# Windowed attention: half-empty key blocks multiplied by the values as pairs of 128x64 array tiles

## The chip, the core and the metric

The kernel runs on one core of one Trainium2 chip. A core has five engines that run at the same time, each through its own list of instructions in order: TensorE (PE, the 128x128 matrix array; the loads of its stationary operand are shown as PEld), VectorE (DVE), ScalarE (ACT), GpSimd (POOL) and SyncE (SP, which here only starts transfers). They synchronise by semaphores. The metric is the device time of one execution in microseconds, taken as the median of several runs. Lower is better.

## What is computed

Four residual layers over x of 2048 tokens by 512 features, in the order A, B, A, B. Both kinds start with a layernorm, have 32 heads of 16 features, and end with a product with `wo` that is added to x. Layer A is linear attention (no mask, all tokens). Layer B is softmax attention in a window of 256 tokens:

```python
x = x + _A_ref(_layernorm(x, axis=-1), A_wqkv, A_wo)
x = x + _B_ref(_layernorm(x, axis=-1), B_wqkv, B_wo)
x = x + _A_ref(_layernorm(x, axis=-1), A_wqkv, A_wo)
x = x + _B_ref(_layernorm(x, axis=-1), B_wqkv, B_wo)
...
# in _B_ref
scores = jnp.einsum("bhqd,bhkd->bhqk", q, k) * (Dh ** -0.5)
mask = (idx[:, None] - idx[None, :] >= 0) & (idx[:, None] - idx[None, :] < W)
scores = jnp.where(mask[None, None], scores, -1e9)
p = _softmax(scores, axis=-1)
o = jnp.einsum("bhqk,bhkd->bhqd", p, v)
```

## The kernel before

The program is a list of operations (`Op`), each with an engine, an emitting function and the tiles it reads and writes. A compressed table in the source (`TABLE`, unpacked in `place`) gives the order of all 2541 operations, the engine of each one that could go to several, and the PSUM bank of each PSUM tile (8 banks of 128 partitions by 512 f32). `synchronise` then derives every semaphore wait from that order. So each engine, and SP's queue of transfers, has a fixed order written out in the table, and nothing is decided at run time.

Tokens are cut into 16 tiles of 128. Layer 1 (A) is built by `layer_a_keys`; layers 2 and 4 (B) by `middle`, in which work of the neighbouring A layers is spread: the output of the A layer before (`a_out`, L406), layernorms (DVE and POOL, then a transposing transfer on SP's queue), and, in layer 2, keys, values and queries of layer 3. `barrier` holds the sums over all tokens that stand between.

In a B layer, for every tile j of 128 tokens:

- `b_qkv` (products L420) makes queries and keys, `b_v` (L406) the values. The keys and values are kept as blocks of 64 keys, and a 128-row operand holds a block for two heads, whose rows alternate. There are therefore 16 head pairs, numbered by f (0 to 3) and gq (0 to 3), and two key blocks, 2j and 2j+1, in each tile.
- `b_scores` (L638, row tiles of 32x128 of the array, four at once) multiplies the key block with up to 256 query columns, and `b_far` (L712 in layer 2, L715 in layer 4, the latter as 32x64 tiles, eight at once) with the last 64 columns of the window. ACT takes the exponential into the buffer P of probabilities (`pb`, `vp`; L648 and L725). The mask is a product or a select on DVE or POOL (L657, L658, L735, L743, L744).
- `b_values` (L764) multiplies probabilities by values. Its stationary operand is a 128x128 piece of P (two heads by 64 keys in the rows, 128 queries in the columns), the moving one 34 columns: 16 value features and a column of ones for each of the two heads. For the 128 queries of tile j, six key blocks matter: 2j-4 to 2j+1. Of the first, only the first 64 queries can see anything, and of the last only the last 64; P holds 64 columns of zeros beside both, so that all six are multiplied as full 128x128 operands. One tile takes 6 x 16 = 96 matmuls, in four operations called `pv` (one for each f, of 24), two of them into one bank.
- DVE divides by the sums (`rcp` L775, `div` L776), the result is transposed (L377 on SP's queue), multiplied by `wo` (L406) and added to x (L574).

The tiles j = 0 and 1 have fewer blocks, and the last tile of layer 4 has its own `b_values_end`. Line numbers are those of the kernel before; in the changed kernel lines from L749 on are moved down.

## Time and profile before

| | |
|---|---|
| median of 3 runs | 408.16 us (406.51 to 409.1) |
| profiled execution, first to last instruction | 405.4 us |
| instructions | 18074 |
| matmuls on PE, busy | 7930, 386.1 us (95%) |
| ACT busy | 341.5 us (84%) |
| DVE busy | 333.6 us (82%) |
| POOL busy | 149.2 us (37%) |

The page gives the span of the profiled execution, and no device time of its own for it; the median of the timed runs is 2.8 us above the span. Busy time is the union of what an engine executes; the matmuls overlap one another, so what one costs is read from start to start, not from its duration. A row of the timeline gives the start, the length from the first start to the last end, and the number of instructions in it. In the rows `128*128`, `32*128` or `32*64` are the rows and columns of the array tile that an instruction uses.

### The profile page before, as it was taken

The numbers are of one execution on the slowest core, as the hardware profiler recorded it, in microseconds if no ns is written. First come the engines' busy times: TensorE is split into PE (matmuls) and PEld (weight loads), VectorE is DVE, ScalarE is ACT, GpSimd is POOL, SyncE is SP. The second block draws the span as 40 slices with busy tenths as digits, with TensorE's granted clock in tenths as the row PEclk, the third lists the DMA queues.
The fourth block names the chain that finished last, engine by engine and source line by source line (L and its number), as shares of the span: only waits on it lengthen the run. The fifth ranks groups of instructions, "written<-read, shape, count | busy, mean of one in ns | idle before, by whom it ended". The sixth has DMA issues, their size and how long they took to land.

```text
span 405.4 us, 18074 instructions
## 1 busy us (share of the span) xinstructions
PE 386.1 (95%) x7930; PEld 263.9 (65%) x8004; DVE 333.6 (82%) x759; ACT 341.5 (84%) x439; POOL 149.2 (37%) x243
## 2 busy tenths in 40 slices
PE   8999999998999999999999999999999999999896
PEld 3644776766576566666666777677767775566665
DVE  6998898979998798887858789997898759776775
ACT  2655568998999999999998445999999999999994
POOL 3555624534363545541752213141132221232212
PEclk9999999999999999999999999999999999999999
DMA  8734216333253545353232000335224433344443
GB/s 250 243 66 128 82 41 127 106 80 92 71 94 69 122 97 101 63 129 81 62 79 56 20 2 12 96 83 135 69 57 108 110 76 75 82 118 94 115 124 107
DMA packets 67062, 37.75 MB, mean 93 GB/s; under 512 B 47688, under 2 KB 62152, under 8 KB 66984
## 3 DMA queue, kind: packets, MB, share of 16 engines
q1 hardware_dynamic: 66640, 35.67, 36.3%
q8 instruction: 63, 1.03, 1.2%
q0 software_dynamic: 336, 0.92, 0.7%
q14 instruction: 15, 0.12, 0.1%
q10 hardware_dynamic: 8, 0.00, 0.0%
HBM read 6.29 MB, written 2.10 MB: 21 GB/s over the span
## 4 chain that ended last, share of the span: by engine, by line
PE 76%; ACT 16%; DVE 5%; issue 2%; DMA 1%; ACTq 0%
PE ps L406 25%; PE ps L420 19%; PE ps L764 13%; ACT pb L648 10%; PE ps L638 6%; PE ps L481 3%; PE ps L715 2%; ACT pb L725 2%; ACT vp L648 2%; PE ps L712 1%; DMA xT<-xn 1%; PE ps L1067 1%; ACT vp L725 1%; PE ps L457 1%; DVE XQ L563 1%
## 5 line engine op out<-in xcount | busy, mean ns | idle before, releaser
L648 ACT ACTIVATE pb<-ps 128x1024 bf16<-128x1024 f32 (+3 forms) x224 | 198.4, 974 | 7.1 <-PE ps L638 5.5
L764 PEld LDWEIGHTS ps<-vB,pb 128*128 128x128 bf16 x2496 | 75.2, 96 | 10.4 <-issue 3.9
L764 PE MATMUL ps<-vB,pb 128*128 128x34 bf16 x2496 | 80.2, 177 | 0.3 <-DVE pb L744 0.2
L420 PE MATMUL ps<-xT,wBp 128*128 128x128 bf16 x1024 | 68.5, 219 | 0.9 <-DMA xT<-xn 0.6
L420 PEld LDWEIGHTS ps<-xT,wBp 128*128 128x128 bf16 x1024 | 58.8, 98 | 10.9 <-issue 4.5
L429 ACT ACTIVATE tE<-ps 128x512 bf16<-128x512 f32 x64 | 37.6, 605 | 26.3 <-PE ps L406 16.5
L743 POOL TENSOR_SCALAR_AFFINE_SELECT pb<-pb 128x1024 bf16<-128x1024 bf16 x32 | 36.9, 1152 | 53.8 <-DVE pb L735 37.6
L657 POOL TENSOR_SCALAR_AFFINE_SELECT pb<-pb 128x512 bf16<-128x512 bf16 x51 | 34.3, 673 | 48.4 <-ACT pb L648 20.6
L725 ACT ACTIVATE pb<-ps 128x1024 bf16<-128x1024 f32 x50 | 49.3, 1052 | 2.0 <-PE ps L715 1.0
L574 DVE TENSOR_TENSOR xres<-ps,xres 128x512 bf16<-128x512 f32 x63 | 42.9, 682 | 9.4 <-PE ps L406 9.1
L370 POOL TENSOR_TENSOR rs<-ve,negh 128x1 f32<-128x1 f32 x64 | 37.2, 581 | 32.1 <-DVE ve L369 27.5
L638 PE MATMUL ps<-XQ,kB 32*128 32x256 bf16 (+3 forms) x992 | 47.0, 264 | 1.7 <-ACT pb L648 0.5
L406 PE MATMUL ps<-wA,XQ 128*128 128x512 bf16 x179 | 45.7, 379 | 1.8 <-issue 0.8
L367 DVE BATCH_NORM_STATS2 stats<-xres 128x6 f32<-128x512 bf16 x64 | 43.8, 686 | 2.7 <-DMA xres<-in_A_x_dram 1.8
L420 PE MATMUL ps<-XQ,wA 128*128 128x128 bf16 x512 | 35.4, 219 | 0.1
L369 POOL TENSOR_SCALAR ve<-mv 128x1 f32<-128x1 f32 x45 | 11.5, 255 | 64.4 <-DVE mv L368 62.4
L420 PEld LDWEIGHTS ps<-XQ,wA 128*128 128x128 bf16 x512 | 30.6, 98 | 5.5 <-issue 0.7
L406 PE MATMUL ps<-wBv,xT 128*128 128x512 bf16 x108 | 30.1, 380 | 2.9 <-issue 1.4
L638 PEld LDWEIGHTS ps<-XQ,kB 32*128 32x128 bf16 x992 | 14.9, 92 | 26.4 <-ACT pb L648 8.4
L406 PE MATMUL ps<-wBo,oT 128*128 128x512 bf16 x103 | 28.6, 380 | 3.1 <-issue 1.9
L406 PE MATMUL ps<-M,XQ 128*128 128x512 bf16 x114 | 29.7, 380 | 1.3 <-issue 0.6
L406 PEld LDWEIGHTS ps<-wA,XQ 128*128 128x128 bf16 x192 | 17.0, 97 | 19.6 <-issue 2.1
(128 smaller groups left out, 569.1 us busy)
## 6 DMA issues: line engine op xcount, KB each, us to landing
vB<-vS SPq DMA_DIRECT2D x64, 136.0 KB, 2.6
kB<-vp SPq DMA_DIRECT2D x64, 128.0 KB, 2.2
wA<-in_A_wqkv_dram SPq DMA_DIRECT2D x3, 512.0 KB, 5.0
out_dram<-xres SPq DMA_DIRECT2D x9, 128.0 KB, 2.8
xres<-in_A_x_dram SPq DMA_DIRECT2D x2, 512.0 KB, 4.9
pb<-in_B_wqkv_dram SPq DMA_DIRECT2D x1, 1024.0 KB, 5.6
out_dram<-xres POOLq DMA_DIRECT2D x7, 128.0 KB, 2.2
xres<-in_A_x_dram SPq DMA_DIRECT2D x3, 256.0 KB, 4.7
```

The source lines that it names most:

```text
L367: self.on("DVE", "stats", lambda e: e.bn_stats(K.stats[:, t, :], K.xres[:, t, :]), key, dve(512), rd=[("xres", t)], wr=[("stats", t)])
L370: self.pow = self.on("POOL", "pow", lambda e: e.tensor_tensor(K.rs[:, t, :], K.ve[:, t, :], K.negh[:], ALU.pow), key + 0.03, (640, 690), r ...
L406: m = e.matmul(K.ps(ps), lhs(c), rhs(c), start=c == 0, stop=c == 3)
L420: m = e.matmul(K.ps(ps)[:, f * P:(f + 1) * P], w(c, f), xT(c), start=c == 0, stop=c == 3)
L429: self.on("ACT", "E", lambda e: e.activation(K.tE[:, s, :], K.ps(ps), ACT.Exp, bias=0.0), key, act(512), wr=[("tE", s)], ps=[ps])
L574: self.on("DVE", "res", lambda e: e.tensor_tensor(K.xres[:, t, :], K.ps(po), K.xres[:, t, :], ALU.add), key, dve(512), rd=[("xres", t)], w ...
L638: m = e.matmul(K.ps(ps[gq])[:, ns * i:ns * i + ns], K.kB[rows, j % 4, 2 * f + b, :, :], K.XQ[rows, f, q:q + ns], start=True, stop=True, ti ...
L648: return e.activation(out(h, ns).rearrange("p (f g) c -> p f g c", f=n), i, ACT.Exp, bias=0.0, scale=0.25)
L657: return e.affine_select(out=x, in_=x, compare_op=ALU.is_ge, fill=0.0, base=1, pattern=[[0, 4 * n], [2, 64]], channel_multiplier=-1)
L725: return e.activation(o.rearrange("p (f g) b c -> p f g b c", g=2), i, ACT.Exp, bias=0.0, scale=0.25)
L743: return e.affine_select(out=x, in_=x, compare_op=ALU.is_ge, fill=0.0, base=-2, pattern=[[0, 16], [-2, 64]], channel_multiplier=1)
L764: m = e.matmul(K.ps(ps)[:, 34 * u:34 * u + 34], K.P((b // 2) % rp)[:, f, gq % 2 * 2 + gq // 2, o:o + P], K.vB[:, (b // 2) % 4, b % 2, r, : ...
```

## The change

For every tile j from 2 on (but for the last of layer 4), `b_pairs` takes the place of `b_values`. The four key blocks that all 128 queries may see, 2j-3 to 2j, are multiplied as before, as full 128x128 operands: four operations of 16 matmuls. The two half-empty blocks are multiplied as pairs: the first 64 queries with block 2j-4 on the array's columns 0 to 63 and the last 64 queries with block 2j+1 on columns 64 to 127, each a 128x64 tile with a stationary operand of 64 columns, adding into partitions 0 to 63 and 64 to 127 of the same bank. That is two operations for each j, one for each half h of the heads, each of 16 matmuls in 8 pairs. Instead of 96 full matmuls a tile j has 64 full ones and 32 on half the columns. In all, 27 tiles (14 in layer 2, 13 in layer 4) and 54 groups of 8 pairs are concerned. The division is moved into a function of its own without a change.

The operations are now 2595, and `TABLE` is a new one: new orders, banks and engines. The order in which the inputs are loaded is kept. Counting the changes between two kinds of array tiles in PE's list gives 329 before and 383 now. Of the operations that can go to several engines, ACT has as many as before (438). DVE has 767 (758 before); among them it takes over six masks of the kind L657/L658 and one of L743/L744 from POOL. POOL has 232 (239 before).

Two places of PE's list follow. The first lies in layer 2. L764 is `b_values`, L638 are scores, L406 products of 512 columns with the weights named. Before:

```order
L764 MATMUL ps<-vB,pb 128x34 x48
L638 MATMUL ps<-XQ,kB 128x256 x8
L406 MATMUL ps<-wBv,xT 128x512 x4
L406 MATMUL ps<-wA,XQ 128x512 x4
L638 MATMUL ps<-XQ,kB 128x256 x8
L764 MATMUL ps<-vB,pb 128x34 x48
L638 MATMUL ps<-XQ,kB 128x256 x8
```

Now, at the same place of PE's list in layer 2 (L765 are the full blocks of `b_pairs`, L783 its pairs):

```order
L765 MATMUL ps<-vB,pb 128x34 x32
L783 MATMUL ps<-vB,pb 64x34 x16
L638 MATMUL ps<-XQ,kB 128x256 x8
L406 MATMUL ps<-wBv,xT 128x512 x4
L406 MATMUL ps<-wA,XQ 128x512 x4
L638 MATMUL ps<-XQ,kB 128x256 x8
L765 MATMUL ps<-vB,pb 128x34 x32
L783 MATMUL ps<-vB,pb 64x34 x16
```

What stood around the group has stayed; 48 full matmuls have become 32 full ones and 16 on half the columns, which stand between them and the scores.

The second place lies in the first half of layer 4, where L715 are the far scores on 32x64 tiles. Before:

```order
L638 MATMUL ps<-XQ,kB 128x224 x8
L764 MATMUL ps<-vB,pb 128x34 x48
L638 MATMUL ps<-XQ,kB 128x224 x8
L420 MATMUL ps<-xT,wBp 128x128 x16
L406 MATMUL ps<-wBo,oT 128x512 x4
L715 MATMUL ps<-XQ,kB 64x64 x64
L764 MATMUL ps<-vB,pb 128x34 x48
L638 MATMUL ps<-XQ,kB 128x224 x8
```

And now:

```order
L638 MATMUL ps<-XQ,kB 128x224 x8
L765 MATMUL ps<-vB,pb 128x34 x32
L783 MATMUL ps<-vB,pb 64x34 x16
L638 MATMUL ps<-XQ,kB 128x224 x8
L406 MATMUL ps<-wBo,oT 128x512 x2
L420 MATMUL ps<-xT,wBp 128x128 x16
L715 MATMUL ps<-XQ,kB 64x64 x64
L406 MATMUL ps<-wBo,oT 128x512 x2
L765 MATMUL ps<-vB,pb 128x34 x32
L783 MATMUL ps<-vB,pb 64x34 x16
L638 MATMUL ps<-XQ,kB 128x224 x8
```

Here the output product L406 has moved ahead by half, and the far scores stand between its halves.

The diff; of the table only the first line of each version is shown:

```diff
--- before.py
+++ after.py
@@ -746,6 +746,58 @@
             engs = {"DVE": dve(1024, "2x"), "POOL": (1260, 1320)}
             self.g.add("mf", engs, mk, key + 1.5 + 0.01 * b, rd=[("F", sl, 0), ("F", sl, 1), ("tri",)] + [("near", sl, b, 0), ("near", sl, b, 2)] * merged, wr=[("F", sl, b, 1)])
 
+    def b_pairs(self, j, key):
+
+        K = self
+        rp = self.rp
+        banks = [Tile(1, K.cls) for _ in range(2)]
+        prob = lambda b, f, gq: K.P((b // 2) % rp)[:, f, gq % 2 * 2 + gq // 2, :]
+        val = lambda b, f, gq: K.vB[:, (b // 2) % 4, b % 2, 4 * f + gq, :]
+        full = ((2 * j, 0), (2 * j - 1, 64), (2 * j - 2, 128), (2 * j - 3, 192))
+        vals = lambda i: [("vB", i % 4, a, b) for a in range(2) for b in range(2)]
+        for f in range(4):
+            def put(e, f=f):
+                m = None
+                for gq in range(4):
+                    u = 4 * (f % 2) + gq
+                    for b, c in full:
+                        o = 384 * (b % 2) + c
+                        m = e.matmul(K.ps(banks[f // 2])[:, 34 * u:34 * u + 34], prob(b, f, gq)[:, o:o + P], val(b, f, gq), start=f % 2 == 0 and gq == 0 and b == 2 * j, stop=False, skip_group_check=True)
+                return m
+            rd = [("F", (j - 2) % rp, h_) for h_ in (0, 1)] + [("F", (j - 2) % rp, 1, 1)]
+            for i, bs in ((j - 2, (1,)), (j - 1, (0, 1)), (j, (0,))):
+                rd += [("P", i % rp, f)] + vals(i)
+                rd += [("P", i % rp, f, b, h_) for h_ in range(3) for b in bs]
+            self.pe("pv", put, key + 0.5 * (f // 2) - 0.001 * (f % 2), 16, 34, rd=rd, ps=[banks[f // 2]])
+
+        for h in range(2):
+            fs = (2 * h, 2 * h + 1)
+
+            def put(e, h=h, fs=fs):
+                m = None
+                for f in fs:
+                    for gq in range(4):
+                        u = 4 * (f % 2) + gq
+                        for half, b in ((0, 2 * j - 4), (1, 2 * j + 1)):
+                            o = 384 if half else 256
+                            m = e.matmul(K.ps(banks[h])[64 * half:64 * half + 64, 34 * u:34 * u + 34], prob(b, f, gq)[:, o:o + 64], val(b, f, gq), start=False, stop=True, tile_position=(0, 64 * half), skip_group_check=True)
+                return m
+            rd = [("F", (j - 2) % rp, h_) for h_ in (0, 1)] + [("F", (j - 2) % rp, 0, 1)] + vals(j - 2) + vals(j)
+            for f in fs:
+                rd += [("P", i % rp, f) for i in (j - 2, j)] + [("P", j % rp, f, 1, h_) for h_ in range(3)]
+            self.pe("pv", put, key + 0.5 * h, 16, 34, mode=(128, 64), occ=256, rd=rd, ps=[banks[h]])
+            self.divide(j, h, key + 0.5 * h, banks[h])
+
+    def divide(self, j, h, key, ps):
+        K = self
+        s = j % 2
+        v = lambda: K.ps(ps)[:, 0:272].rearrange("p (u a d) -> p u a d", u=8, a=2)
+        self.on("DVE", "rcp", lambda e: e.reciprocal(K.rc[:, s, h, :].rearrange("p (u a) -> p u a", a=2), v()[:, :, :, 16]), key + 0.02, dve(16, "recip"), wr=[("rc", s, h)], ps=[ps])
+        self.on("DVE", "div", lambda e: e.tensor_tensor(
+            K.o[:, s, :].rearrange("p (a r d) -> p r a d", a=2, d=DH)[:, 8 * h:8 * h + 8],
+            v()[:, :, :, 0:16], K.rc[:, s, h, :].rearrange("p (u a) -> p u a", a=2).unsqueeze(3).to_broadcast([P, 8, 2, DH]), ALU.mult),
+            key + 0.03, dve(256), rd=[("rc", s, h)], wr=[("o", s, h)], ps=[ps])
+
     def b_values(self, j, h, key):
         K = self
         rp = self.rp
@@ -770,13 +822,7 @@
             if j >= 2:
                 rd += [("F", (j - 2) % K.rp, h_) for h_ in (0, 1)] + [("F", (j - 2) % K.rp, h_, 1) for h_ in (0, 1)]
             self.pe("pv", put, key - 0.001 * (f % 2), 4 * len(blocks), 34, rd=rd, ps=[ps])
-        s = j % 2
-        v = lambda: K.ps(ps)[:, 0:272].rearrange("p (u a d) -> p u a d", u=8, a=2)
-        self.on("DVE", "rcp", lambda e: e.reciprocal(K.rc[:, s, h, :].rearrange("p (u a) -> p u a", a=2), v()[:, :, :, 16]), key + 0.02, dve(16, "recip"), wr=[("rc", s, h)], ps=[ps])
-        self.on("DVE", "div", lambda e: e.tensor_tensor(
-            K.o[:, s, :].rearrange("p (a r d) -> p r a d", a=2, d=DH)[:, 8 * h:8 * h + 8],
-            v()[:, :, :, 0:16], K.rc[:, s, h, :].rearrange("p (u a) -> p u a", a=2).unsqueeze(3).to_broadcast([P, 8, 2, DH]), ALU.mult),
-            key + 0.03, dve(256), rd=[("rc", s, h)], wr=[("o", s, h)], ps=[ps])
+        self.divide(j, h, key, ps)
 
     def b_values_end(self, j, h, key):
 
@@ -815,13 +861,7 @@
             for f in fs:
                 rd += [("P", j % rp, f)] + [("P", j % rp, f, b, k) for b in (0, 1)] + [("P", j % rp, f, b, 2, k) for b in (0, 1)]
             self.pe("pv", put, key - 0.001 * (1 - k), 8, 34, rd=rd, ps=[ps])
-        s = j % 2
-        v = lambda: K.ps(ps)[:, 0:272].rearrange("p (u a d) -> p u a d", u=8, a=2)
-        self.on("DVE", "rcp", lambda e: e.reciprocal(K.rc[:, s, h, :].rearrange("p (u a) -> p u a", a=2), v()[:, :, :, 16]), key + 0.02, dve(16, "recip"), wr=[("rc", s, h)], ps=[ps])
-        self.on("DVE", "div", lambda e: e.tensor_tensor(
-            K.o[:, s, :].rearrange("p (a r d) -> p r a d", a=2, d=DH)[:, 8 * h:8 * h + 8],
-            v()[:, :, :, 0:16], K.rc[:, s, h, :].rearrange("p (u a) -> p u a", a=2).unsqueeze(3).to_broadcast([P, 8, 2, DH]), ALU.mult),
-            key + 0.03, dve(256), rd=[("rc", s, h)], wr=[("o", s, h)], ps=[ps])
+        self.divide(j, h, key, ps)
 
     def b_out(self, j, key, by_pe):
         K = self
@@ -917,8 +957,12 @@
                     self.b_scores(j, b, [f, f + 1], base + j + (f + b) / 4)
             if j + 2 < T:
                 self.b_far(j, base + j + 0.8)
-            for h in range(2):
-                (self.b_values_end if last and j == T - 1 else self.b_values)(j, h, base + j + (h + 1) / 2 + par["k_pv"])
+            end = last and j == T - 1
+            if j >= 2 and not end:
+                self.b_pairs(j, base + j + 0.5 + par["k_pv"])
+            else:
+                for h in range(2):
+                    (self.b_values_end if end else self.b_values)(j, h, base + j + (h + 1) / 2 + par["k_pv"])
             if not last:
                 self.closing = [self.g.ops[-1]]
             k = base + j + 1 + par["k_wo"]
@@ -941,60 +985,61 @@
 
 
 TABLE = (
-    r"c-qx^1GFSt(r#$0ZQHhO+qP}nwr$(CZQHi_XPvtD&h*^wnSO8n_11b>mANZp2fp|sa-YnqbKl)_58WdNK!9-Dg#d<Npdb_oXow5(AUK4EFc2RSKtf0aiNU}f",
...
+    r"c-qx?1K2D{(r#uTBeRcf+qP}nwr$(CZQHhO+qQ1?_s!XznLRr@|6V-Lt**+dj*NKo4OCQDNArbJ!Ie^>RTvdgg;n8H2n8yhis6gti|mW95~zeKyh@}JE3Htm",
...
 )
```

107 lines of the change are left out of this document (54 added, 53 removed).

## The prediction

> **What bounds the kernel now.** I read the page first: the busy shares, the 40 slices, and the chain that ended last.
>
> ```profile
> span 405.4 us, 18074 instructions
> PE 386.1 (95%) x7930; PEld 263.9 (65%) x8004; DVE 333.6 (82%) x759; ACT 341.5 (84%) x439; POOL 149.2 (37%) x243
> ...
> PE   8999999998999999999999999999999999999896
> ...
> ACT  2655568998999999999998445999999999999994
> ...
> PEclk9999999999999999999999999999999999999999
> ...
> PE 76%; ACT 16%; DVE 5%; issue 2%; DMA 1%; ACTq 0%
> ```
>
> PE is over 90% busy in nearly every slice, at full clock, and makes 76% of the chain; ACT makes 16%, some 65 us. ACT is low only in the two A stages (slices 1 to 6 and 23 to 25). The mean hides this, so I asked for the busy time by stage, with the bounds set at the first and last exponential of layers 2 and 4:
>
> ```profile
> 0.00:61.50 61.50, 59.67 (x587) 35.80 (x599) 53.53 (x130) 32.16 (x54) 29.01 (x69) 1.00 0.46 134
> 61.50:223.90 162.40, 155.63 (x3200) 103.92 (x3230) 136.03 (x302) 155.90 (x185) 74.55 (x112) 1.00 0.40 89
> 223.90:256.70 32.80, 32.48 (x551) 24.90 (x555) 28.61 (x62) 15.96 (x30) 8.48 (x15) 1.00 0.05 14
> 256.70:398.60 141.90, 134.67 (x3537) 96.73 (x3556) 112.15 (x260) 135.59 (x168) 34.98 (x44) 1.00 0.40 97
> ```
>
> The columns are the length, then PE, PEld, DVE, ACT and POOL. Both windowed stages, the second and the fourth row, have **two** full engines: PE 155.6 and ACT 155.9 of 162.4 us, PE 134.7 and ACT 135.6 of 141.9 us. The whole change lies in these two stages. Whatever PE saves there, ACT lets through 6.5 us in the one (162.4 - 155.9) and 6.3 us in the other at the very most.
>
> Is PE busy because it is full, or because long latencies overlap? The timeline of a stretch of layer 2 answers that:
>
> ```profile
> 120.83 0.40 PE L638 MATMUL ps<-XQ,kB 32*128 32x256 bf16 x8
> 121.31 1.36 PE L764 MATMUL ps<-vB,pb 128*128 128x34 bf16 x48
> 122.60 0.40 PE L638 MATMUL ps<-XQ,kB 32*128 32x256 bf16 x8
> ...
> 126.03 0.41 PE L712 MATMUL ps<-XQ,kB 32*128 32x64 bf16 x32
> 126.37 0.62 PE L420 MATMUL ps<-xT,wBp 128*128 128x128 bf16 x8
> ```
>
> ```profile
> L764 PEld LDWEIGHTS ps<-vB,pb 128*128 128x128 bf16 x2496 | 75.2, 96 | 10.4 <-issue 3.9 <-POOL pb L657 1.0 <-ACT pb L648 0.9
> L764 PE MATMUL ps<-vB,pb 128*128 128x34 bf16 x2496 | 80.2, 177 | 0.3 <-DVE pb L744 0.2
> L420 PE MATMUL ps<-xT,wBp 128*128 128x128 bf16 x1024 | 68.5, 219 | 0.9 <-DMA xT<-xn 0.6 <-ACT pb L648 0.3
> L712 PE MATMUL ps<-XQ,kB 32*128 32x64 bf16 x448 | 5.8, 189 | 0.2
> ```
>
> One matmul of L764 lasts 177 ns, so the last of the 48 starts at 121.31 + 1.36 - 0.18 = 122.49, and start to start is (1.36 - 0.177) / 47 = **25.2 ns**. The 0.3 us of idle time before 2496 of them says that they hardly ever wait. PE is full in the sense that counts: fewer of them means time on PE.
>
> **The change, part by part.**
>
> *Removed.* In each of the 54 groups (27 tiles, two halves) 16 full matmuls go: of 48 there remain 32. 16 x 25.2 = 403 ns a group.
>
> *Added: eight pairs a group.* No row of before has a 128x64 tile. Two neighbours bound it:
>
> ```profile
> 44.80 0.40 PE L543 MATMUL ps<-XQ,zs 128*32 128x128 bf16 x16
> 301.85 0.27 PE L715 MATMUL ps<-XQ,kB 32*64 32x64 bf16 x16
> 301.85 0.30 PE L715 MATMUL ps<-XQ,kB 32*64 32x64 bf16 x24
> 301.85 0.71 PE L715 MATMUL ps<-XQ,kB 32*64 32x64 bf16 x64
> L543 PE MATMUL ps<-XQ,zs x128: 219/219/219, 44.8 to 306.2; 128*32 128x128 bf16 x128
> L715 PE MATMUL ps<-XQ,kB x896: 184/209/212, 259.7 to 382.3; 32*64 32x64 bf16 x180
> ```
>
> L543 uses four tiles of all 128 rows side by side, each with its own moving columns: 16 matmuls of 128 columns make four rounds in 0.40 us, so a round takes (0.40 - 0.219) / 3 = 60 ns. The single full matmul of 128 columns (L420 above, eight in 0.62 us, 219 ns each) takes (0.62 - 0.22) / 7 = 57 ns. So column tiles do run at once. L715 has stationary operands of 64 columns, two beside each other on the same rows, as the pairs have. The three rows on it are the same operation, cut off after 16, 24 and all 64 matmuls: the third round of eight adds 0.30 - 0.27 = 0.03 us. So two 64-column loads and their 64 moving columns fit into 30 ns; the pair moves only 34. Lower end: 25 ns, the start to start of L764. Upper end: L715 over the whole operation, (0.71 - 0.21) / 7 = 71 ns a round; but such a round issues 16 instructions and a pair's only four. I take **30 ns**, the nearest row: 240 ns a group.
>
> *Added: switches between kinds of tiles.* PE's list has 383 of them instead of 329, one more a group. Their price is in the timeline: from the last L764 at 122.49 to the scores at 122.60 is 0.11 us where 0.025 would do, 85 ns; from the last L712 (126.03 + 0.41 - 0.19 = 126.25) to L420 at 126.37 is 0.12, less one round of 0.03, 90 ns. I take 88 ns. This already includes that the next stationary operand can't be loaded ahead.
>
> Sum for a group: 240 + 88 - 403 = -75 ns. Times 54: **PE -4.1 us**, 2.1 us of it in layer 2 (28 groups) and 1.95 in layer 4 (26). With 25 ns for the pair -6.2 us, with 71 ns +13.7 us.
>
> The Trainium skill, "TensorE: Matmul & The Clock Gate", sections "LDWEIGHTS (loading the stationary operand)" and "Weight-path perf modes — Fast Weight Load (FWL) and DoubleRow", speaks against this change: only an operand of all 128 columns gets the fast load, and any other takes its columns / 1.2 in ns, an estimate of 53 ns for 64 columns. By that rule a group would be 424 + 88 - 403 = +109 ns and PE +5.9 us. The third and second row on L715 disagree: 0.03 us for a round with such loads.
>
> *The other engines.* The table also moves work:
>
> ```profile
> L658 DVE TENSOR_TENSOR pb<-pb,tri 128x512 bf16<-128x512 bf16 x17 | 7.6, 455 | 1.9 <-ACT pb L648 1.9
> L744 DVE TENSOR_TENSOR pb<-pb,tri 128x1024 bf16<-128x1024 bf16 x18 | 12.8, 713 | 0.1
> L395 ACT ACTIVATE vp<-ps 128x512 bf16<-128x512 f32 x4 | 2.4, 606 | 0.0
> L548 ACT ACTIVATE rec<-recf 128x128 bf16<-128x128 f32 x6 | 1.9, 309 | 2.8 <-DVE recf L547 2.8
> ```
>
> DVE takes six masks at 455 ns and one at 713 ns from POOL, +3.4 us, five of the six in layer 2, where it is busy 136 of 162.4 us: hidden. Without that cover, a mask at 0.46 us would stand ahead of the pairs. ACT's sum stays nearly: in layer 2 two value copies more (606 ns each), one 309 ns copy less and an exponential traded with a neighbouring stage, some +0.5 us; in layer 4 one query copy and two transposed copies less, about -1.3 us. The order of SP's queue and of all else is rearranged, but at the two places shown in the section on the change the neighbours have stayed or moved by one row, so I cost the rearrangement at zero, and keep it as a risk.
>
> *Waits.* The pairs need the last scores of block 2j+1 and the far mask of block 2j-4; the full blocks before them don't. So what waits latest now waits at the pairs, behind 32 x 25 = 0.8 us of full blocks. Behind a waiting pair stand the next scores, and behind those ACT. Before, every `pv` operation waited for all six blocks, so no wait is new; it can only come later. The gain is at most what the loads of L764 wait for masks and exponentials now (1.0 + 0.9 us in the row above), the loss nothing. I take zero, the nearer end, since the groups stand where they stood.
>
> *From PE to the end.* In layer 4 ACT needs 135.6 - 1.3 = 134.3 us of a stage that would be 139.9: I count all of the 1.95. In layer 2 ACT needs 155.9 + 0.5 = 156.4 of 160.3, 97.6%; some waiting of ACT for scores will stay, so I count half of the 2.1, 1.05 us. Together **-3.0 us**: the profiled span goes from 405.4 to 402.4, and the median, 2.8 us above the span, from 408.2 to **405.2 us**.
>
> **The rivals.**
>
> *ACT is the bound, and PE's saving vanishes.* For it: ACT 96% in both stages, and its 65 us of the chain. Against it: PE has 76% of the chain and stands before ACT there as well. Time: 408.2 us, give or take 1. The Trainium skill ("Perfetto Trace Analysis", section "Identifying the Most-Contended Engine") would judge PE's headroom by the share of its loads, not of its matmuls; that is 65% here, which points to this rival. The 25.2 ns from start to start and the 0.3 us of waiting say otherwise.
>
> *The pairs are paced by their loads (slower).* Place: the eight pairs of a group. If the loads of 64 columns over all 128 rows are not hidden as those over 32 rows are in L715, a round costs 60 ns (as in L543) to 71 ns. It decides at (403 - 88) / 8 = 39 ns a pair: above that the change loses. At 60 ns a group is +165 ns and the kernel +8.9 us, 417 us; at 71 ns 422 us. Against it: the 0.03 us of the third round. The page's rule above is this rival, and its 53 ns would give 408.2 + 5.9 = 414 us.
>
> *The new order is less tight (slower).* Outside its busy time PE has 162.4 - 155.6 + 141.9 - 134.7 = 14.0 us in the two stages. DVE's added masks in layer 2 are the place where it could grow: 5 x 0.46 = 2.3 us if each stands ahead of a waiting pair, and as much again where ACT then waits for the scores behind the pair: 405.2 + 4.6 = 410 us. If the 14.0 us grow by half, 412 us; beyond that it is 416.
>
> *More than expected.* The pair at 25 ns (PE -6.2 us) and an order that lets ACT use all of it: 402 us.
>
> **How the numbers follow.** Forecast (403.5 to 407) 0.40; ACT as the bound (407 to 409.5) 0.19; more than expected 0.14; less tight (409.5 to 416) 0.18; load-paced (416 and above) 0.09. The range 401.5 to 412.5 leaves out the load-paced case and less than half of "less tight", some 0.17 in all. A difference of under 1% (404.1 to 412.2) can hardly be told from no change in this kernel, whose three runs lie 2.6 us apart. Faster by over 1%: a quarter of the forecast (0.10) and "more than expected", 0.24. Slower by over 1%: load-paced and half of "less tight", 0.18. Within 1%: 0.58.
>
> **What would show it.** A group of pairs in the timeline: 16 matmuls on 128x64 tiles in 7 x 0.03 + 0.18 = 0.39 us; 0.60 us would be the load-paced case. PE's busy time in both windowed stages about 2 us less each, with the stages 1 to 2 us shorter. If the stages keep their length and PE's idle time before the scores grows (released by ACT), ACT is the bound. If PE waits for masks on DVE or POOL ahead of the pairs, the order is less tight. The forecast is wrong if the two windowed stages together do not get shorter by 1.5 to 5 us, or if stages 1 and 3, which have no pairs, change by over 1 us.

## The result and the profile after

The changed kernel takes **411.25 us** (median of six runs, 409.60 to 411.76) beside 407.62 us for the kernel before: a ratio of **1.0093, interval 1.0067 to 1.0119**. By the ratio it is slower by 3.8 us, where 3 us less were forecast. Two executions among all the runs of this document, at granted clocks of 0.66 (514.81 us) and 0.96 (412.32 us), are left out of the ratios. From the page of the changed kernel (span, busy time of each engine, shares of the chain of waits):

```profile
span 409.7 us, 18137 instructions
PE 394.4 (96%) x8004; PEld 260.3 (64%) x8004; DVE 336.5 (82%) x768; ACT 343.0 (84%) x439; POOL 144.6 (35%) x236
...
PE 64%; ACT 13%; DVE 11%; DMA 8%; issue 2%; SPq 1%; POOL 0%; POOLq 0%; DVEq 0%
```

The chain has lost 12 points on PE and won them on DVE and DMA (5% and 1% before): the last end now hangs on transfers and vector work more often. The busy time by stage, with bounds at the first and last exponential of layers 2 and 4 (length, then PE, PEld, DVE, ACT, POOL):

```profile
0.00:63.10 63.10, 60.73 (x602) 35.60 (x603) 53.76 (x132) 32.86 (x56) 29.53 (x70) 1.00 0.52 135
63.10:226.60 163.50, 159.56 (x3240) 102.67 (x3239) 136.35 (x304) 157.18 (x187) 72.57 (x108) 1.00 0.38 87
226.60:259.00 32.40, 32.40 (x542) 24.38 (x540) 28.34 (x62) 16.21 (x30) 6.47 (x12) 1.00 0.07 18
259.00:402.30 143.30, 137.94 (x3554) 94.90 (x3553) 114.52 (x263) 135.75 (x167) 33.84 (x43) 1.00 0.45 95
402.30:409.70 7.40, 3.81 (x78) 2.80 (x74) 3.51 (x10) 0.98 (x2) 2.14 (x4) 1.00 0.31 109
```

The rows of before, with each bound set 0.3 or 0.4 us later than in the prediction:

```profile
0.00:61.80 61.80, 59.97 (x592) 35.89 (x601) 53.83 (x131) 32.16 (x54) 29.31 (x69) 1.00 0.46 134
61.80:224.20 162.40, 155.63 (x3193) 103.95 (x3227) 135.74 (x302) 156.20 (x186) 74.25 (x112) 1.00 0.40 89
224.20:257.10 32.90, 32.42 (x551) 24.93 (x556) 29.00 (x63) 16.06 (x30) 8.48 (x15) 1.00 0.05 14
257.10:398.90 141.80, 134.73 (x3541) 96.87 (x3566) 112.05 (x259) 135.49 (x169) 34.98 (x44) 1.00 0.40 97
398.90:405.40 6.50, 3.32 (x64) 2.27 (x61) 3.00 (x8) 1.61 (x4) 2.15 (x4) 1.00 0.36 121
```

So the 4.3 us between the two profiled spans are **+1.3, +1.1, -0.5, +1.5 and +0.9**: no stage with pairs got shorter, and a third of the loss lies in layer 1, which has no pairs at all. PE's busy sums can't be set against those of before, whose trace lacks 74 of 8004 matmul records.

The pairs themselves, in a stretch of the timeline of layer 4 (start, length from first start to last end):

```profile
381.98 0.20 PE L783 MATMUL ps<-vB,pb 128*64 128x34 bf16 x1
...
382.03 0.18 PE L783 MATMUL ps<-vB,pb 128*64 128x34 bf16 x1
...
382.22 0.18 PE L783 MATMUL ps<-vB,pb 128*64 128x34 bf16 x1
```

From the second to the eighth pair 0.19 us pass: (382.22 - 382.03) / 6 = **32 ns a pair**, beside 30 forecast. By the starts of the matmuls, 16 full blocks and the way out to the scores were 16 x 25.2 + 109 = 512 ns; now, in this group, the way in from the full blocks, the pairs and the way out are 107 + 50 + 6 x 32 + 116 = 465 ns. That saves 47 ns, 2.5 us over 54 groups, not 4.1. The median of the 43 groups that come right behind full blocks is 469 ns beside 510 before, 2.2 us.

What has grown is found in three views. In layer 1, PE's matmuls have two waits (in total, times, longest) that they don't have in the kernel before. The loads of L406 did wait for the same transfers before, 0.6 us, and now wait 1.2:

```profile
PE ps L406 <- DMA XQ<-vp: 0.7, 1, 0.7
PE ps L383 <- DVE vp L371: 0.2, 1, 0.2
```

In layer 2, ACT's copies of values, 1.2 us x2 before, have become four, and its sum has gone from 156.2 to 157.2 us. The stage has gained 1.1 us, but a kernel shown below has the same sum in a stage of 162.6 us:

```profile
L395 ACT ACTIVATE vp<-ps 128x512 bf16<-128x512 f32 x4 | 2.4, 604 | 0.1
```

And in layer 4, PE stops **within** an operation of pairs, after 12 of its 16 matmuls, with no semaphore to wait for ("issue"):

```profile
386.70 0.36 PE L783 MATMUL ps<-vB,pb 128*64 128x34 bf16 x12
387.71 0.24 PE L783 MATMUL ps<-vB,pb 128*64 128x34 bf16 x4 [0.64 <-issue]
```

### The profile page after: what moved, and what is told of

The parts are those of the page before. It is cut to its first block, busy times and chain, and to the rows that moved or that the text cites. A ratio compares the mean times of both kernels' runs of the same rounds, so it can differ in the third digit from the quotient of the medians.

```text
span 409.7 us, 18137 instructions
## 1 busy us (share of the span) xinstructions
PE 394.4 (96%) x8004; PEld 260.3 (64%) x8004; DVE 336.5 (82%) x768; ACT 343.0 (84%) x439; POOL 144.6 (35%) x236
## 4 chain that ended last, share of the span: by engine, by line
PE 64%; ACT 13%; DVE 11%; DMA 8%; issue 2%; SPq 1%; POOL 0%; POOLq 0%; DVEq 0%
PE ps L406 23%; PE ps L420 15%; ACT pb L648 9%; PE ps L765 7%; PE ps L638 6%; DMA xT<-xn 3%; PE ps L783 3%; PE ps L481 3%; ACT pb L725 2%; DVE XQ L563 2%; ACT vp L648 2%; DMA kB<-vp 2%; DVE stats L367 2%; PE ps L715 1%; DMA XQ<-vp 1%
## 5 line engine op out<-in xcount | busy, mean ns | idle before, releaser
L743 POOL TENSOR_SCALAR_AFFINE_SELECT pb<-pb 128x1024 bf16<-128x1024 bf16 x33 | 39.6, 1200 | 48.3 <-DVE pb L735 35.3
L765 PEld LDWEIGHTS ps<-vB,pb 128*128 128x128 bf16 x1536 | 48.6, 96 | 8.6 <-issue 3.0
L765 PE MATMUL ps<-vB,pb 128*128 128x34 bf16 x1536 | 52.7, 177 | 0.0
L574 DVE TENSOR_TENSOR xres<-ps,xres 128x512 bf16<-128x512 f32 x63 | 42.9, 683 | 10.5 <-PE ps L406 10.0
L406 PE MATMUL ps<-wA,XQ 128*128 128x512 bf16 x192 | 49.4, 379 | 1.3 <-DMA XQ<-vp 0.7
L638 PE MATMUL ps<-XQ,kB 32*128 32x256 bf16 (+3 forms) x992 | 47.0, 263 | 3.1 <-DVE o L796 0.8
L657 POOL TENSOR_SCALAR_AFFINE_SELECT pb<-pb 128x512 bf16<-128x512 bf16 x45 | 30.2, 671 | 44.1 <-ACT pb L648 16.8
L406 PE MATMUL ps<-wBv,xT 128*128 128x512 bf16 x128 | 34.9, 381 | 0.0
L406 PE MATMUL ps<-wBo,oT 128*128 128x512 bf16 x124 | 32.8, 381 | 1.0 <-ACT pb L648 0.7
L406 PE MATMUL ps<-M,XQ 128*128 128x512 bf16 x128 | 33.4, 380 | 0.3
L369 POOL TENSOR_SCALAR ve<-mv 128x1 f32<-128x1 f32 x44 | 10.2, 232 | 65.4 <-DVE mv L368 64.0
L638 PEld LDWEIGHTS ps<-XQ,kB 32*128 32x128 bf16 x992 | 15.0, 92 | 28.7 <-ACT pb L648 7.4
L795 DVE RECIPROCAL rc<-ps 128x16 f32<-128x16 f32 x64 | 16.2, 253 | 16.5 <-PE ps L783 14.4
```

What stands on the lines that cost most here:

```text
L406: m = e.matmul(K.ps(ps), lhs(c), rhs(c), start=c == 0, stop=c == 3)
L574: self.on("DVE", "res", lambda e: e.tensor_tensor(K.xres[:, t, :], K.ps(po), K.xres[:, t, :], ALU.add), key, dve(512), rd=[("xres", t)], w ...
L638: m = e.matmul(K.ps(ps[gq])[:, ns * i:ns * i + ns], K.kB[rows, j % 4, 2 * f + b, :, :], K.XQ[rows, f, q:q + ns], start=True, stop=True, ti ...
L657: return e.affine_select(out=x, in_=x, compare_op=ALU.is_ge, fill=0.0, base=1, pattern=[[0, 4 * n], [2, 64]], channel_multiplier=-1)
L743: return e.affine_select(out=x, in_=x, compare_op=ALU.is_ge, fill=0.0, base=-2, pattern=[[0, 16], [-2, 64]], channel_multiplier=1)
L765: m = e.matmul(K.ps(banks[f // 2])[:, 34 * u:34 * u + 34], prob(b, f, gq)[:, o:o + P], val(b, f, gq), start=f % 2 == 0 and gq == 0 and b = ...
```

## The experiments

All ratios are to the kernel before, run beside on the same chip.

### The pairs in the old order, and full blocks in the new one

The first kernel keeps the table of before; the pairs stand inside the second `pv` operation of each group (which makes 14 more switches than the change has). The second keeps the changed table and undoes the pairs:

```diff
+ full = [x for x in blocks if j < 2 or x[1] not in (256, -64)]
...
+ for g in (f - 1, f):
+     for gq in range(4):
+         for half, b in ((0, 2 * j - 4), (1, 2 * j + 1)):
+             m = e.matmul(ps[64 * half:64 * half + 64, ...], ..., tile_position=(0, 64 * half))
```
```diff
- for half, b in ((0, 2 * j - 4), (1, 2 * j + 1)):
-     m = e.matmul(ps[64 * half:64 * half + 64, ...], prob[:, o:o + 64], ..., tile_position=(0, 64 * half))
+ for b, o in ((2 * j - 4, 256), (2 * j + 1, 320)):
+     m = e.matmul(ps[:, ...], prob[:, o:o + P], ...)
```

> The order, banks and engines of before; only the two half-empty blocks are multiplied as pairs, behind the second of the two operations of a group. In the profile of after a group costs 107 + 243 + 116 = 466 ns from its last full matmul to the next kind of tile, where 16 full matmuls and one switch took 403 + 109 = 512 ns: 46 ns a group, 2.5 us in all. Theory 'the new order costs, the pairs gain': 1 to 2.5 us faster than before, ratio 0.994 to 0.998. Theory 'the pairs cost more than their own time': slower than before, ratio 1.005 or more.

> The new order, banks and engines, but the half-empty blocks multiplied as full 128x128 operands again (zeros included), in the operations that held the pairs. Theory 'the new order costs, the pairs gain': 1 to 2.5 us slower than after, 412 to 414 us, ratio to before 1.012 to 1.016. Theory 'the pairs cost more than their own time': as fast as before or nearly, ratio 1.000 to 1.003.

Measured: **0.9997 (0.9975 to 1.0019)** for the pairs in the old order, **1.0089 (1.0058 to 1.0119)** for full blocks in the new one, beside 1.0093 for the change. Both lie between what the two theories expected. The pairs are worth nothing that can be measured in either order, and the loss stays when they are undone: it belongs to the new table with its operations. Another run of the pairs in the old order gave a profile at full clock:

> The pairs in the order of before, a second time, for its profile: the time as before (407 to 408 us); PE's busy time in the two windowed stages about 0.5 us less each, and its waiting more by as much.

```profile
61.70:223.90 162.20, 159.68 (x3226) 102.48 (x3225) 135.64 (x302) 156.21 (x186) 74.11 (x112) 1.00 0.41 89
...
256.90:399.10 142.20, 138.27 (x3568) 95.73 (x3567) 112.16 (x259) 135.58 (x169) 34.98 (x44) 1.00 0.39 97
```

407.33 us in one run; the stages are 0.2 shorter and 0.4 us longer than before. This trace has all 8004 matmuls, and shows PE at 98% and 97% of the two stages: outside its busy time PE has 2.5 + 3.9, some 6.5 us with roundings, where the prediction read 14.0 us from a trace with 74 matmuls missing.

With the pairs as operations of their own in the old order, as the change has them:

> The pairs as operations of their own, as in after, but the order, banks and engines of before for everything else (each group of pairs directly behind its second pair of full operations). If the first run with the old order was right, 407 us, ratio to before 0.998 to 1.002; its profile shows PE with some 2.5 us more idle time in the two windowed stages than before, ACT with the same, and both stages as long as before (162.3 and 141.8 us, within 0.7).

1.0032 (1.0009 to 1.0055), above the expectation: the split into operations of their own, in the old order, already costs a third of the loss. The profile is 0.8 us longer; layer 1 is 0.6 us shorter and layer 4 1.5 us longer (143.3), where this kernel has a stop of 1.1 us behind a group of pairs, of the kind shown above. It comes back below.

### Is it the queue of transfers?

The change moved SP's transfers too. One kernel puts one weight load (`wBo`) back to its old place in SP's queue, the other the whole of SP's queue (order of the entries in the table, nothing else):

> After, but the load of wBo stands at its old place of SP's queue, behind seven more transposing transfers. In after a transposing transfer at 14.7 us takes 5.95 us and PE waits 0.86 us behind it at 20.7 us, while the load runs. Theory 'the load holds up the transfer': 0.8 to 1.2 us faster than after, the end of layer 1 as early as in before. Theory 'layer 1 lost time elsewhere': within 0.3 us of after.

> After, but the whole of SP's queue (loads, transposing transfers, keys and values) in the order of before; PE, ACT, DVE and POOL as in after. The chain of waits of after has six transfers in it, of which PE waits 3 us in all; before had one. Theory 'transfers started late by the new order of SP cost the time': 2.5 to 4 us faster than after. Theory 'the order of PE, ACT and DVE costs it, transfers are only where it shows': within 1 us of after apart from what the load of wBo brings.

1.0140 (1.0103 to 1.0178) and 1.0161 (1.0122 to 1.0199): both **slower** than the change, against the expectation. With `wBo` back alone, layer 1 took 64.5 us: PE waits 2.2 us there for another transposing transfer. The whole old queue did take the loss out of layer 1 (62.2 us instead of 63.1), and layer 4 then took 145.8 us instead of 143.3. Its rows in the timeline and by stretch (the number ahead of the last two is the granted clock):

```profile
358.59 1.69 PE L420 MATMUL ps<-xT,wBp 128*128 128x128 bf16 x16 [2.38 <-DMA xT<-xn]
...
369.00 1.07 PE L420 MATMUL ps<-xT,wBp 128*128 128x128 bf16 x16
```

```profile
358.84:362.26 3.42, 3.09 (x92) 2.40 (x90) 1.69 (x4) 1.44 (x2) 0.00 (x0) 0.50 0.56 117
```

PE waited 2.4 us for a transposing transfer, and for the next 3.4 us its granted clock was **half**: 16 matmuls took 1.69 us there and 1.07 later. So neither result tells what a queue is worth by itself; each move made another transfer late.

### Which part of the table?

> Pairs throughout; order, banks and engines of before up to the first scores of layer 4, those of after from there. After lost 1.4 us in layer 4 and 0.9 behind it against before. Theory 'the loss belongs to the order of each stage': 1.5 to 2.5 us slower than before. Theory 'the loss of layer 4 comes from what the stages before hand over': within 0.7 us of before.

> The changed kernel up to the first scores of layer 4, and from there the order, banks and engines of before, with the pairs as operations of their own in both. The run with the new order in layer 4 alone gave +0.87%. If layer 4's new order carries the loss: 407.5 to 409 us. If the stages before it carry as much again (layer 2 and the linear layers got longer by 1.3 us each in the changed kernel's profile): 409.5 to 411.5 us.

1.0087 (1.0057 to 1.0117) with the new layer 4 alone, 1.0089 (1.0059 to 1.0118) with everything new but layer 4. Each half costs as much as the whole: the loss isn't a sum over places. The profile of the second, layers 2 and 4:

```profile
63.30:225.90 162.60, 159.48 (x3240) 102.64 (x3239) 136.17 (x304) 157.09 (x187) 72.52 (x108) 1.00 0.39 88
...
258.30:401.70 143.40, 138.47 (x3565) 95.76 (x3563) 111.76 (x259) 135.77 (x169) 34.98 (x44) 1.00 0.41 95
```

Layer 2 in the new order, with ACT's two more copies in its 157.1 us, is only 0.2 us longer here than before, and layer 4 in the **old** order 1.6 us longer, 1.1 of it in one stop within an operation. In the profile of the first, the stop in layer 4 is 1.5 us long, and 1.9 us later PE's clock is halved for 3.4 us. Then order and engines apart:

> The changed kernel's order and banks, with full blocks in place of the pairs (as in the run with full blocks in the new order, 411.3 us), but every operation on the engine that it had before (masks, evictions, copies and stores back). If the loss lies in the order and the banks: 410 to 412 us. If it lies in the moved operations (six masks onto DVE, copies between ACT and DVE): 406.5 to 408.5 us.

> The kernel before with its order, banks and full blocks, and the changed kernel's choice of engine for every operation. If the loss lies in the order and the banks: 407 to 408.5 us, as before. If it lies in the moved operations: 410 to 412 us.

**1.0636 (1.0592 to 1.0680) and 1.0619 (1.0577 to 1.0660)**: neither expectation. Either mixture costs 25 us, with the sums of work almost unchanged. The net changes of a few operations hide how much was traded: 102 operations stand on another engine in the two tables, among them 29 masks that went from POOL to DVE and 22 that went back. In the first of these profiles, PE's clock is halved for 10 us in all, which is a part of the 25. ACT's waits for scores, before the exponentials in the new order on the old engines:

```profile
L648 ACT ACTIVATE pb<-ps 128x1024 bf16<-128x1024 f32 (+3 forms) x224 | 199.0, 974 | 18.4 <-PE ps L638 17.7
```

And in the changed kernel:

```profile
L648 ACT ACTIVATE pb<-ps 128x1024 bf16<-128x1024 f32 (+3 forms) x224 | 198.6, 980 | 9.0 <-PE ps L638 8.3
```

That fits operations that stand in the queue of another engine than the order was made for and hold up those behind them; which ones do was not shown. So a rearrangement can't be judged by counting what moved; when order and engines don't belong together, its price reaches 6%.

### What is a microsecond of PE worth?

Half-empty blocks left out altogether (their share is missing in the output), old order, all waits kept; and the other way round, each first block multiplied twice:

```diff
+ blocks = [x for x in blocks if j < 2 or x[1] not in (256, -64)]
```
```diff
- for i, (b, c) in enumerate(blocks):
+ for i, (b, c) in enumerate(blocks[:1] * (j >= 2) + blocks):
```

> The kernel before, whose values operations leave the two half-empty blocks out altogether (part of the output's sum is left out): 32 matmuls a group instead of 48, no pairs, no switch, all waits and the order as before. PE loses 54 x 16 x 25.2 ns = 21.8 us of work, 11.3 us of it in layer 2 and 10.5 us in layer 4; ACT, DVE and POOL keep theirs. Theory A, PE's sum sets the stages (the prediction's step): they get shorter until ACT is full, by 6.5 and 6.3 us at most, so 395 to 399 us. Theory B, the stages are set by waits between PE and ACT in a fixed order, so that most of what one engine saves comes back as waiting: 403 to 406.5 us, and PE's waiting grows by 16 us or more.

> The kernel before, each group with eight matmuls more (the first block of each is multiplied twice, the second time over the first): 54 x 8 x 25.2 ns = 10.9 us more on PE, nothing else. If PE sets the time on this side (it has 14 us outside its busy time in the two stages, and waits for the others little): 414 to 419 us. If the stages have slack for it, as the small gain from less work would have it on the other side: 408 to 410 us.

| on PE | measured | ratio |
|---|---|---|
| 21.8 us less | 403.92 us | 0.9917 (0.9887 to 0.9947) |
| 10.9 us more | 420.22 us | 1.0313 (1.0261 to 1.0366) |

Up and down differ by a factor of six to seven: a microsecond **added** to PE costs 12.7 / 10.9 = 1.2 us (0.0313 x 407, interval 1.0 to 1.4), a microsecond **taken away** gives 3.4 / 21.8 = 0.16 us (interval 0.10 to 0.21). Of the 12.7 us, 1.7 are more stops within operations (below); without them it is 1.0 us for each. So the kernel stands at a corner between two slopes. With 10.5 us less PE work the stage of layer 4 took 142.1 us beside 141.8, but PE's clock was halved for 3.4 us of it. Six executions at full clock have a median of 403.25 us, which is 3.6 us less than the kernel before at full clock: still 0.16. What took PE's place is seen in the kernel with the blocks left out, in its timeline in layer 2 and its waits over the whole span (the second for ACT):

```profile
129.61 5.78 ACT L648 ACTIVATE pb<-ps 128x1024 bf16<-128x1024 f32 x6
...
130.86 0.40 PE L638 MATMUL ps<-XQ,kB 32*128 32x256 bf16 x8 [0.44 <-ACT pb L648]
...
132.70 0.40 PE L638 MATMUL ps<-XQ,kB 32*128 32x256 bf16 x8 [0.47 <-ACT pb L648]
```

```profile
PE ps L638 <- ACT pb L648: 5.9, 18, 0.5
```

```profile
ACT pb L648 <- PE ps L638: 5.4, 10, 1.3
```

PE's scores wait for the exponentials 5.9 us (0.5 us before), while elsewhere in the same run the exponentials wait 5.4 us for scores (5.5 before, so that did not shrink). Each waits for the other, at different places.

### Is ACT the bound, then?

Twelve exponentials of 1024 columns cut to half (part of the softmax is left out), six in layer 2 and six in layer 4, in the kernel before, with the pairs in the old order, and with the blocks left out:

```diff
+ def ex(e, h=h, n=1 if h and b and fs[0] and j in (4, 6, 8, 10, 12, 14) else n):
```

> Before, with 12 exponentials halved (six tiles in layer 2 and six in layer 4; half of the probabilities of those blocks are left out, so part of the softmax is missing). By the durations of before (about 0.96 us for 1024 columns, 0.85 for 896, 0.53 for 512) ACT has 2.6 us less in layer 2 and 2.2 us less in layer 4, PE the same work. Theory 'ACT sets the windowed stages': 3 to 5 us faster than before. Theory 'PE sets them as well': within 1.5 us of before, since PE has 98% of these stages filled.

> The same 12 halved exponentials on top of the pairs in the old order (part of the softmax is left out, as in the run beside it). Theory 'ACT sets the windowed stages, PE has room': as fast as the run with fewer exponentials and no pairs, within 1 us. Theory 'both engines are full, and the pairs only gain once ACT gives way': 2 us or more faster than that run.

> The kernel before with the two half-empty blocks left out (as in the run that gave 0.9917) and also twelve exponentials halved (as in the run that gave 0.9988); part of the output's sums is left out in both ways. PE loses 21.8 us of work, ACT 3.9 us. If ACT is what sets the stages once PE has room, ACT's 3.9 us come through whole: 403.9 - 3.9 = 400 us, ratio 0.982. If what is left is fixed waiting that neither engine's work sets: 403 to 403.5 us, ratio 0.990 or more.

ACT lost 2.1 and 1.8 us of work in the two stages. The times: 0.9988 (0.9965 to 1.0010) in the kernel before, 1.0006 (0.9985 to 1.0028) with the pairs, 0.9874 (0.9828 to 0.9920) with the blocks left out. ACT alone isn't the bound either: 3.9 us less give 0 to 1.4 us, and with them gone the pairs still gain nothing. With PE relieved by 21.8 us, ACT's 3.9 us give 403.9 - 402.4 = 1.5 us, between the two expectations, and the intervals of the two kernels overlap. What can be said is that 26 us less work on the two full engines together make the kernel 5 us faster. With both, layer 4 takes 139.5 us. That the fixed order of hand-overs between the engines holds the rest is the reading that is left; it was not tested.

### Does the new order lose because PE is full?

The changed table, the operation of the pairs cut down to one full matmul (most of the two blocks' share is missing in the output):

> The changed kernel's order, banks and engines, where the operation of the pairs does one full matmul instead of 16 half ones (nearly all of the two half-empty blocks is left out of the output's sums), without a switch: PE has some 20 us less to do than in the changed kernel. If the new order's loss is its own, whatever PE has to do: 403.9 + 3.5 to 4 = 407.5 us. If it comes from how the new order shares a full PE: 404 to 405 us, as with the blocks left out in the old order.

1.0061 (1.0030 to 1.0092), 410.02 us: this is above both expectations. With some 20 us less on PE the new order gains only 1.2 us, and stands 1.4% above the old one with the blocks left out (0.9917); so do the executions at full clock alone (408.8 beside 403.2 us). The loss doesn't come from PE's load. In layer 1 this kernel waits more for the same transfer than the changed one:

```profile
PE ps L406 <- DMA XQ<-vp: 2.0, 2, 1.7
```

### The stops within operations

In each trace I counted PE's instructions (loads, matmuls and the few others, in order) up to each stop of over 0.3 us that no wait explains. Start of the stop, from load to load, its length and the count modulo 256:

```
before                  360.2  0.32 us  193
changed                 362.6  0.47 us  193 | 386.9  0.85 us  193 | 401.6  0.47 us  193
full blocks, new order  363.1  0.56 us  193 | 387.7  0.72 us  193
new layer 4 alone       360.9  0.42 us  193 | 385.2  1.52 us  193
old layer 4 alone       386.2  1.12 us  193
pairs as own operations 384.3  1.11 us  193
first block twice       352.4  0.43 us  193 | 390.3  0.42 us  193 | 395.5  1.13 us  194
pairs, old order        none
```

They all lie at one residue (the count can be off by one). In the stop of the pairs as own operations PE also waited for an exponential that ended 0.5 us before it went on. The page's row of instruction packets of the changed kernel (packets, MB) has 63 of 16 KB on one queue:

```profile
q8 instruction: 63, 1.03, 1.1%
```

Their number goes with PE's count: 63 for 16,225 instructions here, 56 for 14,496 with the blocks left out, 66 for 17,088 with a block doubled, some 258 each time. So PE's code seems to come in pieces of 256 instructions, and the stops to be PE out of code. In the changed kernel the packet ahead of the stop at 386.9 began at 385.14, when PE was 162 instructions past the last boundary, and took 1.26 us; in layers 2 and 4 they mostly begin within 120 instructions of a boundary, 3 to 8 us ahead of the next, and this one 2.6 us ahead. It ended at 386.40, and PE went on 1.3 us later. That holds throughout: of the 29 such stops in the traces here (that of the run at a clock of 0.66 left aside), every one ends 1.2 to 1.6 us after a packet on that queue ended, and where the changed kernel reaches a boundary more than 1.6 us after its packet ended, it crosses it without a stop.

The stops add up to 1.8 us in the changed kernel and 0.3 us before, and the length of layer 4 goes with them. Among the profiles at full clock throughout, three without one there take 142.2, 141.9 and 141.2 us (the last two with 1.8 us less work on ACT; before takes 141.8 with 0.3 us of stops), and six of the whole work with 1.1 to 2.1 us of stops take 143.3 to 143.9 us. Among the six are both orders, and pairs as well as full blocks: the full blocks in the changed operations stop at the same place as the pairs, and the pairs inside the old operations nowhere. To test the mechanism, 48 tiny matmuls at PE's very start, where it waits for the first loads, move the boundaries by 96 instructions:

```diff
  for _ in range(9): e.matmul(PS[:, SPARE, :], warm[:, 0:P], warm, ...)
+ for _ in range(48): e.matmul(PS[:, SPARE, 0:8], warm[:, 0:P], warm[:, 0:8], ...)
```

> The changed kernel with 48 tiny matmuls (8 columns) more at PE's very start, where it waits for the first loads: PE's instructions move by 96 against the boundaries of 256 at which it stops in the middle of operations (0.47 us at 362.6, 0.85 us at 386.9 and 0.47 us at 401.6 in the changed kernel's profile). If these stops come from fetching instructions and are part of the loss: the stops leave these places, and the time falls by up to 1.7 us, to 409.5 to 410.5 us. If they only show a waiting that is there anyway: 411.3 us as before, with the stops at the same places.

> The same shift by 96 instructions in the kernel with the new order in layer 4 alone (410.3 us), whose stops at the boundaries are 1.20 us at 257.2, 0.42 us at 360.9 and 1.52 us at 385.2. If the stops are the loss of this kernel: 407.5 to 408.5 us. If they aren't: 410.3 us.

The same group of pairs in the shifted changed kernel, with its neighbours, and another place in its layer 2:

```profile
391.75 0.18 PE L765 MATMUL ps<-vB,pb 128*128 128x34 bf16 x1
391.86 0.43 PE L783 MATMUL ps<-vB,pb 128*64 128x34 bf16 x16
392.22 0.37 PE L638 MATMUL ps<-XQ,kB 32*128 32x224 bf16 x8
```

```profile
84.00 1.04 PE L406 MATMUL ps<-wBv,xT 128*128 128x512 bf16 x4
86.57 1.04 PE L406 MATMUL ps<-wBo,oT 128*128 128x512 bf16 x4 [1.53 <-DMA oT<-o]
```

The mechanism holds and the gain doesn't. All three stops left their places, and PE's lag behind the changed kernel fell by 0.81 us at the second. But stops of 0.84, 0.59 and 0.57 us came up at the new boundaries (317.6, 329.3 and 350.8 us), the first with a halved clock for 3.4 us right behind it (2.3 us of lag for both), and transfers landed late at other places, as in the row above. The time is **1.0184 (1.0151 to 1.0218)**, some 4 us slower than the changed kernel, of which hardly any (0.2 us) was lost in the first 9 us.

The other kernel gave **1.0187 (1.0145 to 1.0229)**, but it can't be set against the 410.3 us of the new layer 4 alone: its lists follow the old order only up to the first scores of layer 2, and the changed one from there on, and no run has the same lists without the shift. Only its start can be compared, and there 2.5 us went in the first 9 us. Two rows of the same line, here and in the shifted changed kernel:

```profile
6.39 2.29 PE L268 MATMUL ps<-kB 128*128 128x512 bf16 x5
```

```profile
6.32 1.02 PE L268 MATMUL ps<-kB 128*128 128x512 bf16 x4
```

Its matmuls start every 0.43 us until 9.8 us, and every 0.21 afterwards; the full clock is granted from 10.0 us on, and in the shifted changed kernel from 5.2.

How such things add up is seen in the start of PE's k-th load of a stationary operand, changed kernel less before (both have 8004):

```
at (us, before)   15   25   60   90  118  186  253  344  376  397
lag (us)         +0.4 +1.0 +0.8 +0.7 +1.6 +1.9 +2.0 +2.2 +2.5 +3.4
```

It grows in steps, and in between falls by up to 1 us, where the two orders do other things (the k-th load isn't the same operation in both).

## Why the prediction was wrong

*"Fewer of them means time on PE", and "from PE to the end" (-3.0 us).* **This step failed.** That L764 runs from start to start in 25 ns and waits little shows that PE is full; it doesn't show that a shorter list shortens the stage. 21.8 us less gave 3.4, and the 1 to 2.5 us of the pairs gave nothing that can be measured, in the old order, in the new one, and with less work on ACT. All of layer 4's share was counted and half of layer 2's; some 0.16 of it was due. The stage's own idle time (14 us on PE, some 6.5 in a trace with all matmuls) was the wrong measure of slack: after a cut of PE's work, it just grows. That 411.25 us lies within the stated range is luck as far as the forecast goes: its sign was wrong, and the range reached that far only because a part of a rival was taken in.

*"I cost the rearrangement at zero."* **This step failed too, and it carries the loss**: full blocks in the new order are as slow as the change, and the split into operations of their own costs a third of it in the old order. Two places whose neighbours stayed say nothing about 2500 operations. The rival "less tight" had the sign and the size (410 to 416 us, 0.18), but its place, DVE's masks in layer 2, was not found. PE's loads of the scores do wait longer for DVE there (7.0 us beside 2.0), though for other tiles than the masks; the old layer 4 with the new layer 2 has 7.1 us of it in a stage of 162.6 us. What the profile shows is a wait for a transposing transfer in layer 1 (0.7 of 1.3 us), and stops for code in layer 4 (1.8 us beside 0.3; the stage grew by 1.5). That layer 4 grows with such stops is seen in all six kernels with over 1 us of them at full clock; why a new order or a split makes packets and transfers late stays open. So does the cause of the 1.1 us in layer 2: ACT's two more value copies have that size (its sum grew by 1.0 us where +0.5 was forecast), but with the same sum the stage can be 162.6 us long. The 0.9 us at the end has no cause here.

*The pair at 30 ns.* Right: 32 ns. The bounds 25 and 71 held, and the rival "paced by their loads" is out. The Trainium skill ("TensorE: Matmul & The Clock Gate", "LDWEIGHTS (loading the stationary operand)") gives columns / 1.2, an estimate of 53 ns for 64 columns. Two such loads and their matmuls start every 32 ns here, so the rule doesn't hold for these tiles side by side.

*The sum for a group, -75 ns.* Right sign, too large: 47 ns in the group shown, 41 by the median. The eight pairs at 32 ns are 256 instead of 240 ns. The added switch is some 112 ns instead of 88: the way in takes 82 ns more than a start without a change, the first pair 20 more than the others, and the way out to the scores some 10 more than before.

*"ACT is the bound, and PE's saving vanishes" (408.2 us, 0.19).* Right about the pairs (0.9997 in the old order), wrong about the reason: 3.9 us less on ACT gave next to nothing. The Trainium skill ("Perfetto Trace Analysis", "Identifying the Most-Contended Engine") would judge PE by the share of its loads, 65% here. Little came of taking PE work away, which agrees with a PE that has headroom; but each microsecond of work added cost 1.2, which does not.

*Waits: zero; DVE's masks hidden.* No new wait at the pairs and none for the masks was seen, but the scores wait longer for DVE's other work, as said above.

*"Wrong if the two stages do not get shorter by 1.5 to 5 us, or if stages 1 and 3 change by over 1 us."* Both came true: the two grew by 2.6 us, and stage 1 by 1.3.

## What to carry to other kernels

Where two engines stand at 96% of a stage, taking work off one of them can gain little (here 3.4 of 21.8 us), and adding some can cost in full: measure both slopes (leave a piece of work out, do a piece twice) before building a faster piece. A new table of orders is a change of its own. Here it cost 0.3 to 1.9%, and 6% when order and engines were mixed, through things that no count of instructions shows, such as when a transfer lands or a piece of code arrives; none of the tables tried here won. So the new piece is first measured in the old order, and the new order with the old piece.

## What the runs showed of the hardware

- Two 128x64 array tiles side by side, each with its own stationary operand of 64 columns and 34 moving columns, start every 32 ns. A full 128x128 with 34 columns starts every 25 ns, so a pair on half tiles saves 18 ns of two full ones, and one more change of the tile shape takes two thirds of it back.
- PE's code arrives in transfers of 16 KB, one for some 256 instructions, each taking 0.9 to 1.6 us. When one begins late, PE stops in the middle of an operation for 0.3 to 1.5 us, at the same count modulo 256, and goes on 1.2 to 1.6 us after a transfer's end (29 stops in the traces here); moving the count moved the stops. Why some transfers of code begin late (2.6 us ahead of the boundary at the long stop of the changed kernel, where most begin 3 to 8) stays open; no run here shows it.
- The granted clock of PE falls to 0.5 for 3.41 us within some executions. The profiles show it of seven kernels: the old queue of SP, the new layer 4 alone, the blocks left out in either order, both mixtures, and the shifted changed kernel. On the chip of both mixtures, 15 executions of the kernel before at a mean clock of 0.999 or more have a median of 406.8 us, and four at 0.995 or 0.996 one of 409.6. It came behind a wait for a transfer (2.4 us) or a stop for code (0.84 and 1.52 us) in three of these profiles, but not behind the stops of 1.1 us; no run shows what sets it off.
- 48 tiny matmuls at the start, 1.4 us of PE's time where it would have waited, moved the end of the changed kernel by 4 us, 2.3 of them by one stop for code with a halved clock behind it.
